# Two key-weight transfers of two rows, the first tile and the constants on another queue, and one low part ahead of another

## The chip, the core and the metric

The kernel runs on one core of a Trainium2 chip. The metric is the device time of one execution in microseconds, the median over the runs. A profiled execution is a run of its own, with its own time.

## What is computed

The input x has 2048 rows of 512. It is normalised row by row, and two branches work on the result xn:

```python
xn = layernorm(x)
# branch A: linear attention, 32 heads of 16
q, k, v = split(xn @ wqkv)
phi_q = [softmax(q @ w_phi), softmax(-q @ w_phi)]      # per head
phi_k = [softmax(k @ w_phi), softmax(-k @ w_phi)]
s = (phi_q @ (phi_k.T @ v)) / (phi_q @ sum(phi_k)) @ wo
# branch B: a gated feed-forward part, 1376 wide
g = silu((relu(xn @ W_gate) * (xn @ W_up)) @ W_down)
out = x + s * g
```

All of it is float32. Matrix products are made from high and low parts: a float32 operand is split into a part rounded to the fast matmul type and the rest, and three products (low times high, high times low, high times high) are added up. The function mm3 writes these three for each slice k of the contraction.

## The kernel before

The rows are taken in 16 tiles of 128. For each tile the kernel normalises, transposes (tile pxT, then XT in high and low part), and multiplies by the key, value and query weights (pk, pv, pq). All weights of the feed-forward branch and the second half of attention follow later; the change touches nothing of them.

Since w_phi acts per head, it is folded into the key and query weights at the start: fold(w, raw, k) multiplies row slice k of the transposed weight (wkT or wqT, tile wk_raw or wq_raw) by the block-diagonal constants bd_sb (named cb in the profile) on TensorE, four matmuls in the program, eight in the trace, into PSUM tile pfold. It returns a function that splits the outcome: ScalarE copies the high part (wkh), VectorE subtracts it for the low part (wkl). The four slices of the key weight are the four "rows" that this text speaks of; each row is 128 partitions of 512 numbers. In DRAM wkT is 128 x 4 x 512, so that a partition's rows lie behind each other, 8 KB in all.

The order of instructions on each engine is the order of the program; a helper (class InOrder, line 52) issues every one of them, which is why nearly all rows of the profile name L52. Transfers are issued by SyncE's queue (SPq) in program order, and each takes the semaphore of the eighth transfer before it, whose landing it waits for. GpSimd issues accumulating transfers on a queue of its own.

The start, lines 829 to 880, is written out by hand: first the loads, then norm_vector(0) with the statistics of the first tile (bs, bm, br on VectorE and GpSimd), the folds of key rows 0 and 1, norm_vector_apply(0) (xn), the split of row 0, the transposes of the first tile with its high part by ScalarE (turn(0, False)), the split of row 1, the folds of rows 2 and 3, then lo_xt, which subtracts on VectorE for the low part of XT, the remaining splits, the second tile's statistics between them, and the product pk of the first tile. In pk's order the first matmul of each slice reads the low part of XT with the high part of the weight; the second reads the high part of XT with wkl; the third both high parts.

Of the kernel before, what the change touches and what calls it, by code (L numbers as in the profile page):

```python
# [13 lines left out]
P = 128  # L14
# [5 lines left out]
KD = D // P  # L20
# [128 lines left out]
def layer_kernel(ctx: ExitStack, tc: tile.TileContext, x, wkT, wqT, wv, wo, wf, cst, out):  # L149
    pace = Clock()  # L150
    nc = InOrder(tc, pace)
# [7 lines left out]
    def u8(shape, name, dt=F32):  # L159
        return sb.tile(list(shape), dt, tag="u8", bufs=B8, name=name)  # L160
# [4 lines left out]
    def u2(shape, name, dt=F32):  # L165
        return sb.tile(list(shape), dt, tag="u2", bufs=B2, name=name)
# [7 lines left out]
    def f32(t):  # L174
        return t.bitcast(F32)

    def add(engine, o, a, b, op=ALU.add):
        engine.tensor_tensor(o, a, b, op=op)
# [31 lines left out]
    N = len(order)  # L210
    X = {}

    def load_x(n):
        b, i = order[n]
        t = b * TPB + i
        X[n] = u2((P, D), "xt")
        nc.sync.dma_start(X[n], x[t * P:(t + 1) * P, :])


    def w_tile(name):  # L220
# [5 lines left out]
    def fold(w, raw, k):  # L226

        p = ps(name="pfold")
        for j in range(KD):
            nc.tensor.matmul(p[:, j * P:(j + 1) * P], raw[:, j * P:(j + 1) * P], bd_sb[:, j, :],  # L230
                             start=True, stop=True)
        return lambda: split(*w[k], p)
# [44 lines left out]
    def transpose_x(n):  # L277
        p = ps((P, 2, 2, P), name="pxT")
        xn = XN.pop(n)
        for k in range(KD):  # L280
            transpose(p[:, k // 2, k % 2, :], xn[:, k * P:(k + 1) * P])
        return p

    def xt_parts(n, s):

        if n % 2 == 0:
            return [(XT[:, A11:A12 + 1, s, :, cols(n)], slice(0, 2))]
        if n not in A21:
            A21[n] = u2((P, 2, 2, P), "a21", F32R)
        return [(A21[n][:, s], 0), (XT[:, A22, s, :, cols(n)], 1)]  # L290

    def hi_xt(n, p):
        for to, c in xt_parts(n, 0):
            nc.scalar.activation(to, p[:, c], AF.Copy)

    def full_xt(n, p):
        XF[n] = u2((P, 2, 2, P), "xf")
        nc.scalar.activation(XF[n], p, AF.Copy)

    def lo_xt(n, p):  # L300
        for (to, c), (hi, _) in zip(xt_parts(n, 1), xt_parts(n, 0)):
            add(nc.vector, to, p[:, c], f32(hi), ALU.subtract)

    def turn(m, full=True):
        p = transpose_x(m)
        hi_xt(m, p)
        if full:
            full_xt(m, p)
        return m, p
# [519 lines left out]
    wk_raw, wv_raw, wq_raw = u8((P, KD, D), "wkT"), u8((P, KD, D), "wvr"), u8((P, KD, D), "wqT")  # L829
    bd_sb = u2((P, KD, P), "cb")  # L830
    ident = sb.tile([P, P], F32, name="ident")
    load_x(0)
    nc.sync.dma_start(bd_sb, cst[:, :KD, :])
    for k in range(KD):
        nc.sync.dma_start(wk_raw[:, k, :], wkT[:, k, :])
        if k == 0:
            nc.sync.dma_start(ident, cst[:, KD, :])
    load_x(1)
    nc.sync.dma_start(wq_raw[:, 0:2, :], wqT[:, 0:2, :])
    nc.sync.dma_start(wv_raw[:, 0:2, :], wv[:, 0:2, :])  # L840
    nc.sync.dma_start(wq_raw[:, 2:4, :], wqT[:, 2:4, :])
    load_x(2)
    nc.sync.dma_start(wv_raw[:, 2:4, :], wv[:, 2:4, :])
    for n in range(3, 7):
# [11 lines left out]
    norm_vector_apply(0)  # L856
    folds[0]()
    px = turn(0, False)
    folds[1]()
    folds = [fold(WK, wk_raw[:, k, :], k) for k in range(2, KD)]  # L860
    lo_xt(*px)
    folds[0]()
    norm_vector(1)
    folds[1]()
# [9 lines left out]
    px = turn(1)  # L874
# [288 lines left out]
```

## Time and profile before

| what | value |
|---|---|
| median of 3 runs | 585.73 us (585.71 to 586.2) |
| the profiled execution, own time | 586.47 us |
| its span, first to last instruction | 584.7 us |
| TensorE busy in the span | 572.5 us (98%) |
| VectorE, ScalarE, GpSimd busy | 395.4, 288.6, 390.2 us |
| SyncE's queue, moved | 125.66 MB |

In the profile PE is TensorE, PEld its weight loads, DVE VectorE, ACT ScalarE, POOL GpSimd, SP SyncE; a q behind an engine is its instruction queue, which issues transfers. Rows of a timeline give the start and the length in microseconds, then the operation as output<-inputs, and in brackets the idle time of that engine before it with what ended it. The chain of waits follows the work that ended last back from the last instruction.

### The profile page before, as it was taken

What the parts mean: (1) busy time and instruction counts of PE and PEld (TensorE: products, weight loads), DVE (VectorE), ACT (ScalarE), POOL (GpSimd) and SP (SyncE); (2) the same over time, 40 slices, a digit from 0 to 9 for tenths busy, and PEclk for the clock granted to TensorE, in tenths of its full rate; (3) what the DMA queues carried; (4) which work ended last, traced back from release to release, by engine and by line L of the source; (5) the groups of instructions that cost most, each with busy time, mean ns of one, the idle gap of its engine ahead of it and who ended that gap; (6) DMA issues with size and microseconds to landing.
All of it is one profiled execution on the core that took longest, in us unless ns stands there. A gap on an engine that the chain in (4) does not pass through costs nothing.

```text
span 584.7 us, 8483 instructions
## 1 busy us (share of the span) xinstructions
PE 572.5 (98%) x2764; PEld 478.0 (82%) x2764; DVE 395.4 (68%) x604; ACT 288.6 (49%) x529; POOL 390.2 (67%) x341
## 2 busy tenths in 40 slices
PE   4999999999999999999999999999999999999997
PEld 4788888888888888888888888888888888888886
DVE  2898765876647976787784532488788868673323
ACT  3798786864635356245434151153554545534510
POOL 0669987998866576997967342544457585775394
PEclk9999999999999999999999999999999999999999
DMA  8358897974698938978967999995576475669863
GB/s 289 112 150 223 221 307 233 265 222 126 164 279 272 347 95 261 301 263 293 283 215 226 319 389 398 315 390 193 130 266 170 137 227 169 183 206 275 254 176 113
DMA packets 82844, 138.26 MB, mean 236 GB/s; under 512 B 7664, under 2 KB 30576, under 8 KB 81904
## 3 DMA queue, kind: packets, MB, share of 16 engines
q1 hardware_dynamic: 79488, 125.66, 64.3%
q0 software_dynamic: 3312, 12.06, 10.8%
q8 instruction: 22, 0.36, 0.3%
q14 instruction: 22, 0.18, 0.1%
HBM read 77.14 MB, written 52.69 MB: 222 GB/s over the span
## 4 chain that ended last, share of the span: by engine, by line
PE 97%; DMA 1%; ACT 1%; DVE 1%; SPq 0%; issue 0%; POOL 0%; POOLq 0%
PE py L52 21%; PE pd L52 10%; PE pa L52 10%; PE pc L52 10%; PE pso L52 8%; PE pk L52 8%; PE pq L52 7%; PE pv L52 7%; PE pb L52 5%; PE pkv L52 3%; PE pnum L52 3%; PE ppT L52 2%; PE pxT L52 1%; PE pfold L52 1%; DMA wkT<-wkT 1%; PE pkb L52 0%
## 5 line engine op out<-in xcount | busy, mean ns | idle before, releaser
L52 PE MATMUL pa<-XT,wa 128*128 128x512 f32 x264 | 68.9, 393 | 0.0
L52 PE MATMUL py<-fdh,hl 128*128 128x512 f32 x176 | 68.8, 391 | 0.0
L52 PE MATMUL py<-fdh,hh 128*128 128x512 f32 x176 | 68.6, 390 | 0.0
L52 PE MATMUL py<-fdl,hh 128*128 128x512 f32 x176 | 68.5, 389 | 0.0
L52 POOL TENSOR_TENSOR hl<-e,hh 128x512 fp32r<-128x512 f32 x22 | 28.4, 1292 | 56.5 <-ACT hh L52 56.2
L52 PEld LDWEIGHTS pa<-XT,wa 128*128 128x128 f32 x264 | 48.5, 188 | 9.4
L52 ACT ACTIVATE hh<-e 128x512 fp32r<-128x512 f32 x22 | 13.9, 632 | 72.1 <-DVE e L52 67.4
L52 POOL TENSOR_TENSOR phl<-ek,phl 128x1024 fp32r<-128x1024 f32 x15 | 36.1, 2403 | 17.9 <-ACT phl L52 17.9
L52 POOL TENSOR_TENSOR hl<-u,hh 128x512 fp32r<-128x512 f32 x22 | 28.5, 1296 | 27.1 <-ACT hh L52 24.8
L52 DVE TENSOR_TENSOR y<-py,y 128x512 f32<-128x512 f32 x40 | 27.5, 689 | 27.2 <-PE py L52 27.1
L52 POOL TENSOR_TENSOR y<-y,ys 128x512 f32<-128x512 f32 x24 | 31.1, 1297 | 17.0 <-ACT ys L52 17.0
L52 PEld LDWEIGHTS py<-fdh,hh 128*128 128x128 f32 x176 | 33.0, 188 | 7.0
L52 PEld LDWEIGHTS py<-fdl,hh 128*128 128x128 f32 x176 | 33.0, 188 | 6.7
L52 PEld LDWEIGHTS py<-fdh,hl 128*128 128x128 f32 x176 | 33.1, 188 | 6.7
L52 POOL TENSOR_TENSOR ez<-eq,zB 128x1024 f32<-128x1024 f32 x16 | 38.4, 2405 | 0.0
L52 DVE TENSOR_TENSOR pTl<-ppT,pTh 128x512 fp32r<-128x512 f32 x32 | 22.1, 690 | 23.1 <-ACT pTh L52 22.7
L52 PE MATMUL pd<-XT,wd 128*128 128x512 f32 x132 | 34.9, 395 | 0.0
L52 PE MATMUL pd<-XT,wc 128*128 128x512 f32 x132 | 34.5, 392 | 0.0
L52 PE MATMUL pb<-XT,wb 128*128 128x512 f32 x132 | 34.5, 393 | 0.0
L52 PE MATMUL pc<-XT,wb 128*128 128x512 f32 x132 | 34.3, 391 | 0.0
L52 POOL TENSOR_TENSOR ol<-of,oh 128x1024 fp32r<-128x1024 f32 x8 | 19.4, 2431 | 22.2 <-ACT oh L52 15.3
L52 PE MATMUL pc<-XT,wc 128*128 128x512 f32 x132 | 34.1, 391 | 0.0
(163 smaller groups left out, 1632.8 us busy)
## 6 DMA issues: line engine op xcount, KB each, us to landing
zacc<-ek POOLq DMA_DIRECT2D x15, 512.0 KB, 5.2
xts<-XT SPq DMA_DIRECT2D x4, 1792.0 KB, 11.3
XT<-xts SPq DMA_DIRECT2D x7, 1024.0 KB, 15.8
wa<-ws SPq DMA_DIRECT2D x26, 256.0 KB, 5.3
wb<-ws SPq DMA_DIRECT2D x26, 256.0 KB, 5.3
wc<-ws SPq DMA_DIRECT2D x26, 256.0 KB, 4.9
rawg<-wf SPq DMA_DIRECT2D x22, 256.0 KB, 3.9
ws<-wa SPq DMA_DIRECT2D x22, 256.0 KB, 3.9
```

Of the source, the lines that this page charges most:

```text
L52: return self.tc.keep_in_program_order(op(*a, **k))
```

## The change

The key weights come in two transfers of two rows each (4 KB a partition) in place of four of one row (2 KB); they are now first on SyncE's queue. The first tile, the constants bd_sb and the identity are issued by ScalarE, in this order, ahead of its first own instruction. On VectorE, the low part of the first tile is put ahead of the low part of key row 1.

```diff
-    def load_x(n):
+    def load_x(n, queue=nc.sync):
...
-        nc.sync.dma_start(X[n], x[t * P:(t + 1) * P, :])
+        queue.dma_start(X[n], x[t * P:(t + 1) * P, :])
...
-    load_x(0)
-    nc.sync.dma_start(bd_sb, cst[:, :KD, :])
-    for k in range(KD):
-        nc.sync.dma_start(wk_raw[:, k, :], wkT[:, k, :])
-        if k == 0:
-            nc.sync.dma_start(ident, cst[:, KD, :])
+    load_x(0, nc.scalar)
+    for k in (0, 2):
+        nc.sync.dma_start(wk_raw[:, k:k + 2, :], wkT[:, k:k + 2, :])
+    nc.scalar.dma_start(bd_sb, cst[:, :KD, :])
+    nc.scalar.dma_start(ident, cst[:, KD, :])
     load_x(1)
...
     folds[0]()
     px = turn(0, False)
+    lo_xt(*px)
     folds[1]()
     folds = [fold(WK, wk_raw[:, k, :], k) for k in range(2, KD)]
-    lo_xt(*px)
     folds[0]()
```

By the order of instructions, TensorE's first matmul now waits for the first two-row transfer and for cb; its fifth in the program, which waited for a row of its own, waits no more. The fold of row 2 waits for the second two-row transfer. On VectorE one subtraction changes place with another; on ScalarE three transfer issues stand ahead of its table load; TensorE's order is the same.

## The prediction

> **What bounds the kernel now.** I read four views in this order: the page for the whole, a table of TensorE's busy time by stretch, the chain of waits through the start, and the timeline of the start with its transfers.
>
> ```profile
> span 584.7 us, 8483 instructions
> PE 97%; DMA 1%; ACT 1%; DVE 1%; SPq 0%; issue 0%; POOL 0%; POOLq 0%
> core 0: us, PE busy (x), PEclk, DMA share, GB/s
> 0.00:7.06 7.06, 0.00 (x1) 1.00 0.67 178
> 7.06:11.46 4.40, 4.40 (x21) 1.00 1.00 375
> 11.46:13.44 1.98, 1.98 (x17) 1.00 1.02 410
> 13.44:14.25 0.81, 0.00 (x2) 1.00 1.05 422
> 14.25:26.20 11.95, 11.20 (x68) 1.00 0.34 128
> 26.20:584.70 558.50, 554.94 (x2663) 1.00 0.76 238
> ```
>
> TensorE carries 97% of the chain that ended last. After 26.20 us it is idle for 558.50 - 554.94 = 3.56 us in all. So behind 26.20 the change, which edits only what comes before, can give nothing of its own; a shift of TensorE's work at 26 us is carried to the end, since what follows waits for events and not for the clock on the wall. TensorE's idle time ahead of that is 7.06 us before its first matmul, 0.81 us from 13.44 to 14.25, and 0.75 us later. The change works on the first two. The chain of waits says what ended them:
>
> ```profile
> 1.65 5.27 DMA wkT<-wkT
> 6.92 0.14 issue
> 7.06 3.75 PE pfold L52 x16
> ...
> 12.81 0.69 DVE wkl L52
> 13.51 0.61 DVE XT L52
> 14.11 0.14 issue
> 14.25 3.01 PE pk L52 x12
> ```
>
> The first gap ends with the landing of the first key-weight row, 5.27 us after its issue; TensorE starts 0.14 us later. The second ends with VectorE: it takes the weight row's low part (wkl) and only then the low part of the first tile (XT), and the product pk, whose first matmul reads that low part, starts 0.14 us after it.
>
> **The low part moved ahead (call it A).** The timeline, VectorE's and ScalarE's rows (start, length, what, idle time before and what ended it):
>
> ```profile
> 11.70 0.60 ACT L52 ACTIVATE XT<-pxT 128x512 fp32r<-128x512 f32 x1 [1.96 <-PE pxT L52]
> 12.19 1.08 ACT L52 ACTIVATE wkh<-pfold 128x512 fp32r<-128x512 f32 x2
> 12.81 0.69 DVE L52 TENSOR_TENSOR wkl<-pfold,wkh 128x512 fp32r<-128x512 f32 x1 [2.35 <-ACT wkh L52]
> 13.42 0.68 DVE L52 TENSOR_TENSOR XT<-pxT,XT 128x512 fp32r<-128x512 f32 x1
> 14.02 0.68 DVE L52 TENSOR_TENSOR wkl<-pfold,wkh 128x512 fp32r<-128x512 f32 x1
> 15.62 0.68 DVE L52 TENSOR_TENSOR wkl<-pfold,wkh 128x512 fp32r<-128x512 f32 x1
> 16.64 0.39 PE L52 MATMUL pk<-wkl,XT 128*128 128x512 f32 x1
> ```
>
> VectorE stood idle 2.35 us until 12.81, waiting for wkh of row 1. What XT's low part reads, its high part by ScalarE, was there at 11.70 + 0.60 = 12.30. Swapped, XT's low part runs from 12.32 to 13.00, and wkl of row 1 follows at 12.93 (operations there start 0.61 apart), where it was to start at 12.81 before: nothing is lost to that wait, and from 12.93 on VectorE's list (wkl of row 2, the second tile's statistics, wkl of row 3) runs 0.47 us earlier than now: 13.42 + 0.61 = 14.03 was the start of wkl of row 2, and becomes 13.54. With 13.00 + 0.14 = 13.14, pk no longer waits for VectorE; TensorE is done with the last fold at 13.44 and goes on at once. That takes the 0.81 us gap away. What is late next: the eleventh of pk's twelve matmuls reads wkl of row 3. It started at 16.64, 2.39 after pk's start, so is now due at 13.44 + 2.39 = 15.83. That wkl starts 0.47 earlier, at 15.15, ends at 15.83, and reaches TensorE 0.14 later, 15.97. So about 0.1 us is given back: A = 0.7 us. Between pk and 26 us ScalarE's copies hang on TensorE's folds and VectorE's operations on those, so they move along. Bounds for A: 0.47, if all that follows goes by VectorE's list, and 0.81.
>
> **The loads (B): when TensorE starts.** The issues, landings and rates of before; the column behind the size is the time from issue to landing, each transfer asked for alone in order of issue:
>
> ```profile
> xt<-x SPq DMA_DIRECT2D x1, 256.0 KB, 2.7
> cb<-cst SPq DMA_DIRECT2D x1, 256.0 KB, 2.9
> 1.18 0.42 SPq L52 DMA_DIRECT2D cb<-cst  x1
> DMA packets 259, 0.47 MB, mean 364 GB/s; under 512 B 28, under 2 KB 28, under 8 KB 259
> DMA packets 714, 1.12 MB, mean 233 GB/s; under 512 B 74, under 2 KB 202, under 8 KB 714
> DMA packets 229, 0.85 MB, mean 423 GB/s; under 512 B 19, under 2 KB 19, under 8 KB 229
> wqT<-wqT SPq DMA_DIRECT2D x2, 512.0 KB, 7.3
> DMA packets 253, 0.46 MB, mean 228 GB/s; under 512 B 30, under 2 KB 30, under 8 KB 253
> wor<-wo SPq DMA_DIRECT2D x1, 256.0 KB, 5.2
> ```
>
> The four rates are of the stretches 2.3 to 3.6 us (the tile and the constants), 3.6 to 8.4 (mostly the four key-weight rows), 9.5 to 11.5 (two-row loads of the query weights, issued between 3.6 and 8.4, and of the value weights with them) and 224.4 to 226.4 (a row of wo, cut like a key row, issued near 223 and landed 5.2 us later). One-row loads, 2 KB pieces 8 KB apart, move at 228 to 233 GB/s both times; two-row loads, 4 KB pieces with the same 8 KB between their starts, at 423. The layouts of wkT and wqT are the same, so I take 423 for the new key loads.
>
> Against that stands what must have landed before the first matmul: now the tile, the constants cb and one row; then cb and two rows, on two queues. How two queues share the engines is seen where GpSimd's accumulating transfer runs beside a spill on SyncE's queue, 104 to 106 us:
>
> ```profile
> q0 software_dynamic: 87, 0.36, 91.5%
> q1 hardware_dynamic: 85, 0.04, 10.7%
> ```
>
> 87 packets against 85, though those of q0 carry nine times the bytes: turns go by packet. So eight 4 KB packets of the first two rows alternate on each engine with eight 2 KB packets of the tile, and the next eight, of rows 2 and 3, with those of cb. The constants, second on ScalarE's queue, land only with the fourth row: after 4 x 0.262 MB of weights beside the 0.524 MB of tile and constants. Now cb lands at 1.18 + 2.9 = 4.08 with tile and constants alone ahead of it; then it lands at 4.08 + 1.049 MB / 423 GB/s = 6.56, and TensorE starts 0.14 later, at 6.70 instead of 7.06. B = 0.36 us. The constants, not the key rows, are then what it waits for.
>
> In the Trainium skill, "DMA: Bandwidth & Descriptors", section "Issuing engines are not separate DMA queues", says that transfers from several engines run on the same 16 DMA engines and interleave, and that a second issuer saves only issue time. The rows agree that they interleave; by that rule the second queue itself is worth nothing, and what gain there is comes from the longer pieces.
>
> B's bounds: if the two-row loads go at the 233 GB/s of one-row loads, cb lands at 4.08 + 4.50 = 8.58, the start is 8.72 and B = -1.66. If turns went by bytes instead, cb would wait for two rows only, 4.08 + 0.524 / 423 GB/s = 5.32, the start is 5.46 and B = +1.60. I stay near 0.36, as the 423 comes from the same layout on the same queue 5 us later.
>
> What else moves and costs nothing: the tile shares its turn with two rows and lands about 0.524 MB / 423 GB/s = 1.24 us later than its 0.75 + 2.7.
>
> ```profile
> 3.49 0.69 DVE L52 BATCH_NORM_STATS2 bs<-xt 128x6 f32<-128x512 f32 x1 [2.61 <-DMA xt<-x]
> 5.26 0.55 DVE L52 TENSOR_SCALAR xn<-xt,bm,br 128x512 f32<-128x512 f32 x1 [0.68 <-POOL br L52]
> 0.75 1.28 ACT L52 ACT_TABLE_LOAD   x1 [0.75 <-PEq L1155]
> 9.14 0.60 ACT L52 ACTIVATE wkh<-pfold 128x512 fp32r<-128x512 f32 x1 [7.11 <-PE pfold L52]
> ident<-cst SPq DMA_DIRECT2D x1, 64.0 KB, 5.0
> ```
>
> Its normalisation took from 3.49 to 5.81, so would end near 7.1, and the transposes that read it come 3.6 us after TensorE's start, at 10.3: 3 us of cover. The identity, third on ScalarE's queue, follows cb by eight short packets in turns with SyncE's, under 2 us, and is wanted at the same 10.3. Rows 2 and 3 are wanted 4.4 us after the start. ScalarE issues three transfers (about 0.45 us each, as SyncE's cb shows) before its table load, which then ends near 3.4; its first work is 2 us after TensorE's start. On SyncE's queue the later loads move up by five issues, and each transfer still waits for the eighth before it; those now land earlier, so the second tile and the query and value weights are not later than now.
>
> **The sum.** 0.7 + 0.36 = 1.06 us. The profiled execution took 586.47 us (its span 584.7 and 1.8 around it), so it would take 585.4; that execution lies 0.74 above the median of the plain runs, 585.73. Against the median: 584.7 us.
>
> **The rivals.**
> *The start gains nothing, A alone.* The first sixteen fold matmuls took 3.75 us and the next sixteen, from 11.46 to 13.44, 1.98, though the granted clock is printed as 1.00 for both. If that change of pace stays at its place in time, work pulled ahead by 0.36 us is done at half the pace, so B is worth 0.18 and the time is 584.85; if cb is late by 0.36 it is A alone, 585.0. In the Trainium skill, "TensorE: Matmul & The Clock Gate", section "Part 1: The HAM clock gate (the "warmup" mystery)", has a half clock at the start and a free-running window of about 3.4 us that ends it; by that rule the change of pace need not follow the start. The trace shows the two paces, not which of both holds. Chance 0.20.
> *The constants come late, slower.* Packets in turns put four rows ahead of cb, where one row was ahead of the start. Should the 233 GB/s of the key weights belong to this place and not to the 2 KB pieces, TensorE starts at 8.72 and the time is 585.73 + 1.66 - 0.7 = 586.7. It decides once TensorE starts later than 7.06 + 0.7 = 7.76. For it: 3.6 to 8.4 is the only stretch of key rows. Against it: the wo row, in another place, at 228, and the two-row loads at 423. Chance 0.17.
> *Turns by bytes, or cb early.* TensorE starts at 5.46: 585.73 - 0.7 - 1.60 = 583.4. The 87 to 85 packets speak against it. Chance 0.08.
> *It does nothing at the end*, because VectorE or GpSimd hold the stretch up to 26 us: 585.7. For it: GpSimd and VectorE take turns there; against it: ScalarE's and VectorE's rows there wait for TensorE's folds. Chance 0.05.
>
> **How the numbers follow.** The forecast has 0.50, with its own range 584.2 to 585.2 (B from 0.1 to 0.8, A from 0.5 to 0.8). About what a measurement of this kernel can tell from no change is 0.2%, 1.17 us: faster means under 584.56. The forecast lies just short of it; I give faster three fifths of its half, 0.30, as packets of two queues may overlap a little, and add the 0.08 of the early constants: 0.38. Slower, over 586.90, is most of the late constants, since 586.7 is close to it, and little else: 0.12. The rest, 0.50, is within. The range leaves out the far ends of the early and the late case: 583.5 to 586.6.
>
> **What would show it.** In the changed profile, TensorE's first fold starts at 6.7, right behind a landing of cb, not of wkT; the issues' table has wkT from issue to landing at under 5.5 us for 512 KB; VectorE's order is XT, wkl, wkl with no wait of pk on VectorE's XT, and the gap of 0.81 us ahead of pk is under 0.15; pk of the second tile starts near 25.1 instead of 26.2, and the rest of TensorE's rows keep their lengths. The forecast is wrong if the first fold starts past 7.8, if pk's gap stays, or if the idle time after 26 us differs from 3.6 us by more than half a microsecond.

## The result and the profile after

The changed kernel took 587.02 us (median of 13 runs, 586.37 to 587.97). The kernel before, run beside it, took 586.2 us (13 runs, 584.78 to 586.67); the 585.73 us told above is the median of the first three of these. The ratio is 1.002, with a 95% interval of 1.0012 to 1.0028: slower, and above the predicted range of 583.5 to 586.6. The profiled execution took 587.09 us with a span of 585.3, against 586.47 and 584.7.

The chain of waits of the changed kernel through the start (start, length, what):

```profile
1.18 6.78 DMA cb<-cst
7.96 0.14 issue
8.09 3.76 PE pfold L52 x16
11.85 0.85 PE pxT L52 x4
12.70 1.87 PE pfold L52 x16
14.57 2.30 PE pk L52 x10
16.87 0.04 issue
16.91 0.73 PE pk L52 x2
17.64 1.80 PE pfold L52 x16
```

TensorE starts at 8.09 us where it started at 7.06, and now the constants cb release it, not a weight row. From there on everything is quicker: pk of the first tile follows the folds with no wait, and ends at 17.64, 9.55 us after the first fold; before it ended at 17.26, 10.20 us after. So the start lost 1.03 us and the low part won 0.65.

The timeline of the changed kernel shows the new order on VectorE and what pk waits for now:

```profile
5.95 0.69 DVE L52 BATCH_NORM_STATS2 bs<-xt 128x6 f32<-128x512 f32 x1 [5.08 <-DMA xt<-x]
13.37 0.69 DVE L52 TENSOR_TENSOR XT<-pxT,XT 128x512 fp32r<-128x512 f32 x1 [1.87 <-ACT XT L52]
13.97 1.28 DVE L52 TENSOR_TENSOR wkl<-pfold,wkh 128x512 fp32r<-128x512 f32 x2
16.18 0.68 DVE L52 TENSOR_TENSOR wkl<-pfold,wkh 128x512 fp32r<-128x512 f32 x1
16.91 0.19 PEld L52 LDWEIGHTS pk<-wkl,XT 128*128 128x128 f32 x1 [0.46 <-DVE wkl L52]
26.59 0.48 PE L52 MATMUL pk<-wkh,a 128*128 128x512 f32 x1
```

XT's low part comes first. The wait that is left is the one of the eleventh matmul, on wkl of row 3, at 16.91. The second tile's pk starts at 26.59 instead of 26.20. Behind it nothing changed, as the row of TensorE's stretches shows (busy time in the second number; idle 558.71 - 555.04 = 3.67 us, before 3.56):

```profile
core 0: us, PE busy (x), PEclk, DMA share, GB/s
26.59:585.30 558.71, 555.04 (x2663) 1.00 0.75 237
```

The transfers of the changed kernel: the rate from 2.3 to 3.6 us, with the two queues' packets (q1 is SyncE's, q10 ScalarE's), then the rates from 3.6 to 5.0 and from 5.0 to 6.5; then the issues in order, with the time from issue to landing behind the size.

```profile
DMA packets 114, 0.36 MB, mean 280 GB/s; under 512 B 0, under 2 KB 0, under 8 KB 114
q1 hardware_dynamic: 64, 0.26, 68.3%
q10 hardware_dynamic: 50, 0.10, 26.5%
DMA packets 152, 0.40 MB, mean 287 GB/s; under 512 B 21, under 2 KB 21, under 8 KB 152
DMA packets 217, 0.62 MB, mean 416 GB/s; under 512 B 16, under 2 KB 16, under 8 KB 217
wkT<-wkT SPq DMA_DIRECT2D x1, 512.0 KB, 5.0
wkT<-wkT SPq DMA_DIRECT2D x1, 512.0 KB, 6.4
xt<-x ACTq DMA_DIRECT2D x1, 256.0 KB, 5.2
cb<-cst ACTq DMA_DIRECT2D x1, 256.0 KB, 6.8
```

64 packets of one queue beside 50 of the other carry 0.26 and 0.10 MB: turns go by packet, and the queue with the longer pieces gets the bytes. cb, with the tile ahead of it on its queue, lands 6.8 us after its issue, where it took 2.9 before. In the stretch in which the first two rows and the tile should have moved at 423 GB/s, the rate was 280, and 287 up to 5.0 us. From there it was 416, while the second pair of rows, which lies in DRAM like the first, was still moving.

### The profile page after: what moved, and what is told of

It is laid out like the page before. It is cut to its first block, busy times and chain, and to the rows that moved or that the text cites. A ratio compares the mean times of both kernels' runs of the same rounds, so it can differ in the third digit from the quotient of the medians.

```text
span 585.3 us, 8477 instructions
## 1 busy us (share of the span) xinstructions
PE 572.7 (98%) x2764; PEld 478.4 (82%) x2764; DVE 395.4 (68%) x604; ACT 288.5 (49%) x529; POOL 390.2 (67%) x341
## 4 chain that ended last, share of the span: by engine, by line
PE 97%; DMA 1%; ACT 1%; DVE 1%; POOL 0%; issue 0%; ACTq 0%; POOLq 0%
PE py L52 21%; PE pa L52 10%; PE pd L52 10%; PE pc L52 10%; PE pso L52 8%; PE pk L52 8%; PE pq L52 7%; PE pv L52 7%; PE pb L52 5%; PE pkv L52 3%; PE pnum L52 3%; PE ppT L52 2%; PE pfold L52 1%; DMA cb<-cst 1%; PE pxT L52 1%; PE pkb L52 0%
```

## The experiments

Fourteen kernels were run. For each: the median and that of the kernel before beside it, the ratio, and from its profile the start of TensorE's first fold and of the second tile's pk. From that pk to the end of the span every profile has 558.45 to 558.78 us, so the last column stands for the whole of the profiled execution. That is one execution and need not be a middle one: e4's took 587.96 us, the longest of its eleven. The experiments ran on four chips, so a difference between two of them is best read through the kernel before beside each.

| kernel | us | before | ratio (95%) | first fold | second pk |
|---|---|---|---|---|---|
| changed | 587.02 | 586.2 | 1.002 (1.0012 to 1.0028) | 8.09 | 26.59 |
| e1 low part alone | 585.39 | 586.07 | 0.9989 (0.998 to 0.9998) | 5.95 | 24.44 |
| e2 loads alone | 587.68 | 586.07 | 1.0027 (1.0016 to 1.0038) | 8.68 | 27.56 |
| e3 constants first | 585.73 | 586.07 | 1.0005 (0.9996 to 1.0015) | 6.04 | 25.14 |
| e4 one queue | 586.82 | 586.07 | 1.0017 (1.0009 to 1.0026) | 9.00 | 27.50 |
| e5 rows contiguous | 584.34 | 586.02 | 0.997 (0.9958 to 0.9981) | 6.12 | 24.72 |
| e6 rows padded | 584.17 | 586.02 | 0.9967 (0.9954 to 0.9979) | 5.94 | 23.86 |
| e7 pairs contiguous | 585.79 | 586.02 | 0.9995 (0.9986 to 1.0004) | 7.34 | 25.74 |
| e8 rows, two queues | 586.23 | 586.02 | 1.0 (0.9991 to 1.0008) | 7.46 | 25.95 |
| e9 tile after row | 583.72 | 585.79 | 0.9962 (0.9949 to 0.9975) | 4.28 | 23.08 |
| e10 pairs, one queue | 586.16 | 585.79 | 1.0003 (0.9995 to 1.0012) | 7.79 | 26.27 |
| e11 tiles ahead | 588.36 | 585.79 | 1.0041 (1.0029 to 1.0053) | 9.73 | 28.21 |
| e12 constants on SyncE | 584.41 | 585.79 | 0.997 (0.9959 to 0.9981) | 5.66 | 24.16 |
| e13 pairs padded | 586.56 | 585.77 | 1.0013 (1.0004 to 1.0022) | 7.63 | 26.43 |
| e14 changed again | 587.24 | 585.77 | 1.0023 (1.0014 to 1.0032) | 8.09 | 26.54 |

### The two parts, each alone

e1 is the kernel before with the low part moved:

```diff
     px = turn(0, False)
+    lo_xt(*px)
     folds[1]()
     folds = [fold(WK, wk_raw[:, k, :], k) for k in range(2, KD)]
-    lo_xt(*px)
```

> The loads as before, only the first tile's low part ahead of the low part of key row 1. Theory (the reordering gains, the loads lose more): TensorE starts at 7.0 to 7.1 as before, the gap of 0.81 us ahead of pk is under 0.15, and from the first fold to the end of pk it takes 9.55 us as in the changed kernel, where before took 10.20; the second tile's pk starts near 25.6; the time is 0.65 us under before. Rival (the reordering is lost or hurts, because the last matmuls of pk now wait for row 3's low part): the second tile's pk starts at 26.2 or later and the time is that of before or above.

e2 is the changed kernel with that undone:

```diff
     px = turn(0, False)
-    lo_xt(*px)
     folds[1]()
     folds = [fold(WK, wk_raw[:, k, :], k) for k in range(2, KD)]
+    lo_xt(*px)
```

> The loads as in the changed kernel, the low parts in the order of before. Theory (the loads cost): TensorE starts near 8.1, behind the landing of the constants, 1.0 us later than before; the gap of 0.8 us ahead of pk is there again; the second tile's pk starts near 27.2 and the time is 1.0 to 1.5 us over before. Rival (the loss came from elsewhere, from the reordering or from the second queue by itself): start near 8.1 but a time within 0.4 us of before, or a start near 7.1.

The chain of waits of e1, and its rate from 3.6 to 8.4 us:

```profile
5.95 3.75 PE pfold L52 x16
9.70 0.85 PE pxT L52 x4
10.56 2.09 PE pfold L52 x16
12.64 2.85 PE pk L52 x12
15.50 1.80 PE pfold L52 x16
DMA packets 798, 1.25 MB, mean 261 GB/s; under 512 B 95, under 2 KB 223, under 8 KB 798
```

pk ends 15.50 - 5.95 = 9.55 us after the first fold, as in the changed kernel. The low part alone is worth 0.65 us by the profiles and 586.07 - 585.39 = 0.68 by the medians. The loads alone cost 587.68 - 586.07 = 1.61, somewhat over the 1.0 to 1.5 that was expected, and in e2's chain the wait ahead of pk is back:

```profile
1.18 7.37 DMA cb<-cst
14.18 0.69 DVE wkl L52
14.87 0.61 DVE XT L52
```

The two parts are two effects with opposite signs. e1 also shows how far one profile can be trusted: its loads are those of the kernel before, and its first fold is at 5.95, not 7.06.

### The order on ScalarE's queue

e3 is the changed kernel with the constants ahead of the tile.

```diff
-    load_x(0, nc.scalar)
+    nc.scalar.dma_start(bd_sb, cst[:, :KD, :])
+    load_x(0, nc.scalar)
...
-    nc.scalar.dma_start(bd_sb, cst[:, :KD, :])
```

> The changed kernel, but on ScalarE's queue the constants go ahead of the first tile. Theory (turns by packet: the constants were late because all four key rows were ahead of them): the constants land with the first two rows, at 5.0 to 5.8, TensorE starts at 5.2 to 6.0; the first tile now lands where the constants did, near 8.0, its normalisation ends near 10.3, and the transposes, wanted 3.6 us after the start, wait for it by 0.5 to 1.5 us; the time is 0.5 to 1.5 us under before. Rival (the start of the transfers is slow whatever comes first): the constants land past 7, and the time is that of the changed kernel or above.

The tile in its chain of waits, and two rows of its timeline:

```profile
1.18 6.78 DMA xt<-x
6.04 3.78 PE L52 MATMUL pfold<-cb,wkT 128*128 128x128 f32 x16 [6.04 <-DMA cb<-cst]
10.37 0.89 PE L52 MATMUL pxT<-ident,xn 128*128 128x128 f32 x4 [0.54 <-DVE xn L52]
```

With one transfer less ahead of cb, TensorE starts 2.05 us earlier; the tile, now second, lands at 1.18 + 6.78 = 7.96 by its chain, exactly where cb landed in the changed kernel, and the transposes wait 0.54 us for it. The median is 1.29 under the changed kernel's, and 0.34 under the kernel before beside it, where 0.5 to 1.5 was expected. Its twelve runs lie in two groups, eight at 585.39 to 585.9 and four at 587.12 to 587.56; the profile is of the first, and what parts them is not known. In the profile the lateness belongs to the second place on ScalarE's queue, whatever stands there.

### One queue or two, one row or two

e4 puts all on SyncE's queue in the order of before, with two-row transfers and the low part moved. e8 is the changed kernel with four one-row transfers.

```diff
 e4, against e1
-    for k in range(KD):
-        nc.sync.dma_start(wk_raw[:, k, :], wkT[:, k, :])
+    for k in (0, 2):
+        nc.sync.dma_start(wk_raw[:, k:k + 2, :], wkT[:, k:k + 2, :])
 e8, against the changed kernel
-    for k in (0, 2):
-        nc.sync.dma_start(wk_raw[:, k:k + 2, :], wkT[:, k:k + 2, :])
+    for k in range(KD):
+        nc.sync.dma_start(wk_raw[:, k, :], wkT[:, k, :])
```

> All loads on SyncE's queue again in the order of before, the key rows in two transfers of two rows, the low parts in the changed order. Theory (order on two queues is to blame, two-row pieces are as fast as those of the query weights, 423 GB/s): the constants land at 4.1 as before, the first two rows at 5.3, TensorE starts at 5.5, the time is 1.6 + 0.65 = 2.2 us under before. Rival (key rows that lie 8 KB apart are slow when they come first, in pieces of 2 or of 4 KB: 233 to 257 GB/s as in both kernels until 4.6 to 8 us): the first two rows land at 6.1 to 6.5, TensorE starts at 6.3 to 6.7 and the time is 1.0 to 1.4 us under before. Should two rows in one transfer make the first fold wait for more than they save, it starts at 7.06 or later and the time is 0.6 under before at the most.

> The changed kernel with its two queues, but the key rows come in four transfers of one row, 2 KB pieces 8 KB apart. Theory (turns go by packet): eight packets of the tile and eight of the constants alternate with eight of row 0 and eight of row 1, so the constants land with the second row, at half the weight bytes of the changed kernel: 5.6 if nothing is slow, 6.2 to 7.2 with the slow start seen so far; TensorE starts 0.14 later and the time is 0.2 to 1.2 us under before, and in any case under that of the changed kernel. Rival (turns by bytes, or the second queue itself delays the constants): the constants land past 7.4 and the time is that of the changed kernel.

The chain of waits of e4, its rate from 4 to 6 us, and the chain of e8:

```profile
1.66 7.20 DMA wkT<-wkT
DMA packets 99, 0.30 MB, mean 149 GB/s; under 512 B 6, under 2 KB 29, under 8 KB 99
```

```profile
1.18 6.15 DMA cb<-cst
```

With e1 and the changed kernel that makes a square, all four with the low part moved: 585.39 (one queue, one row), 586.82 (one queue, two rows), 586.23 (two queues, one row), 587.02 (both). Two rows in one transfer cost 1.43 us on one queue and 0.79 on two; the second queue costs 0.84 with single rows and 0.20 with pairs. Against the kernel before beside each, the four are -0.68, 0.75, 0.21 and 0.82 us, so the costs become 1.43, 0.61, 0.89 and 0.07. The pairs are a loss by themselves, as the intervals show on one queue and on two. The second queue with single rows probably is one too (the intervals of e1 and e8 overlap by a hair); with pairs it costs nothing that can be seen. e4 came out as the last of its three cases, a start past 7.06 and no more than 0.6 us gained. In e8 the constants landed at 1.18 + 6.15 = 7.33, between what theory and rival had; it beats the changed kernel, but the gain over the kernel before did not come. e4 has no second queue, so TensorE waits for the weights: twice the bytes must land before the first fold, and they moved at 149 GB/s.

### The layout of the key weights in DRAM

Is it the place in time or the layout that makes them slow? In e5 each row (of e1's loads) lies contiguous in DRAM; in e6 the 2 KB pieces lie 8704 bytes apart instead of 8192; e7 is the changed kernel with each pair of rows contiguous; e10 is e4 with contiguous pairs; e13 is the changed kernel with its 4 KB pieces 8704 bytes apart, and e14 the changed kernel again beside it. The host only stores the same numbers elsewhere.

```diff
 e5
-        nc.sync.dma_start(wk_raw[:, k, :], wkT[:, k, :])
+        nc.sync.dma_start(wk_raw[:, k, :], wkT[k])
 e6
+        nc.sync.dma_start(wk_raw[:, k, :], wkT[:, k, :D])
 e7, e10
+        nc.sync.dma_start(wk_raw[:, k:k + 2, :], wkT[k // 2])
 e13
+        nc.sync.dma_start(wk_raw[:, k:k + 2, :].rearrange("p k d -> p (k d)"), wkT[:, k // 2, :2 * D])
```

> The loads and queue of before, the low parts in the changed order, but wkT lies in DRAM row after row: each of the four transfers reads 256 KB in one piece instead of 128 pieces of 2 KB that start 8 KB apart. Theory (the 8 KB between the pieces makes the start slow: in before, the changed kernel and the one-queue kernel alike the key rows move at 170 to 260 GB/s until some 5 to 8 us): the first row lands at 4.7 to 5.0, 3.2 us after its issue instead of 4.2 to 5.3, TensorE starts at 4.9 to 5.2, from 3.6 to 8.4 us the rate is 380 to 420 GB/s, and the time is 2.4 to 2.8 us under before (1.9 to 2.1 from the start, 0.65 from the low part). Rival (the place is slow, first transfers after the constants, whatever they read): the first row lands at 5.8 to 6.9 as in the two kernels with one-row loads, the rate stays at 230 to 260 GB/s, and the time is 0.7 under before.

> As the kernel with contiguous rows, but wkT keeps its layout with every row padded by 128 bytes: the pieces are 2 KB as in before and start 8704 bytes apart instead of 8192. Theory in its narrow form (it is the round distance of 8192, under which all pieces of a row fall in the same place of some pattern of the memory): as contiguous, first row landed at 4.7 to 5.0, TensorE started at 4.9 to 5.2, time 2.4 to 2.8 us under before. Theory in its wide form (any scattered pieces are slow): first row landed at 5.8 to 6.9, time 0.7 under before. The constants, whose 2 KB pieces start 4608 bytes apart, landed without delay, which speaks for the narrow form.

> The changed kernel with its two queues, but wkT lies in DRAM as two pairs of rows, each pair 512 KB in one piece. Theory (two faults of the forecast are apart: the order of turns put the constants behind all four rows, and that was foreseen at 1.57 MB and full rate; the slow start of rows 8 KB apart was not): the constants land with the last rows at 6.2 to 6.7 and TensorE starts at 6.3 to 6.8, as forecast for the changed kernel; the time is 0.9 to 1.4 us under before. Rival (two queues at the start are slow by themselves): the constants land past 7.4 and the time is that of before or above.

> All loads on SyncE's queue in the order of before, key rows in two transfers of two rows, low parts in the changed order, and wkT in DRAM as two contiguous pairs. Theory (two rows in one transfer cost for two reasons that can be told apart: the first fold waits for twice the bytes, some 0.65 us at full rate, and the scattered rows were slow in that kernel, 170 GB/s at 4 to 6 us): the first pair lands at 5.4 to 6.2, TensorE starts at 5.5 to 6.4, the time is 1.0 to 2.0 us under the one-queue kernel with scattered pairs (586.8), so 584.8 to 585.8. Rival (the slow start is not of the layout): TensorE starts past 7, time 586.3 or more.

> The changed kernel with its two queues, the pairs of rows still in 4 KB pieces, but these start 8704 bytes apart instead of 8192. Theory (the round distance of 8192 is what made the changed kernel's start slow): constants landed near 7.2 and TensorE started near 7.3, as with contiguous pairs on two queues; over 300 GB/s from 2.3 to 3.6 us; time 1.0 to 1.4 us under the changed kernel run beside it. Rival (pieces that are scattered at all are slow): constants landed near 8, TensorE started near 8.1, under 290 GB/s from 2.3 to 3.6 us, time within 0.4 us of the changed kernel.

> The changed kernel as it is, beside the padded one on the same chip. All theories: constants landed at 7.6 to 8.3, TensorE started at 7.8 to 8.4, time 0.7 to 1.2 us over before.

The medians fall in every pair: e1 to e5 by 1.05 us, e1 to e6 by 1.22, changed to e7 by 1.23, e4 to e10 by 0.66, e14 to e13 by 0.68. Against the kernel before beside each, that is 1.00, 1.17, 1.05, 0.38 and 0.68. The 0.38 of e10 is not shown, as its interval overlaps that of e4; e13 and e14 ran side by side on one chip, and e14's median lies above the highest run of e13. The rates, in the order e5 and e6 (3.6 to 8.4 us), e7 (2.3 to 3.6), e13 (2.3 to 3.6, then 3.6 to 5.0), e10 (4 to 6):

```profile
DMA packets 855, 1.40 MB, mean 291 GB/s; under 512 B 94, under 2 KB 222, under 8 KB 855
```

```profile
DMA packets 843, 1.36 MB, mean 284 GB/s; under 512 B 92, under 2 KB 220, under 8 KB 843
```

```profile
DMA packets 153, 0.48 MB, mean 365 GB/s; under 512 B 0, under 2 KB 0, under 8 KB 153
```

```profile
DMA packets 111, 0.35 MB, mean 269 GB/s; under 512 B 0, under 2 KB 0, under 8 KB 111
DMA packets 217, 0.58 MB, mean 414 GB/s; under 512 B 31, under 2 KB 31, under 8 KB 217
```

```profile
DMA packets 238, 0.57 MB, mean 285 GB/s; under 512 B 22, under 2 KB 110, under 8 KB 238
```

Contiguous pairs went at 365 where scattered ones went at 280, and on one queue at 285 where e4 had 149. The padded pairs of e13 were still slow up to 3.6 us (269) and then went at 414, where the changed kernel had 287; the start came 0.46 us sooner (7.63 against 8.09), and the 0.68 us lie between what the two theories expected. e14 itself came to 1.47 over the kernel before, above the 0.7 to 1.2 that was expected.

The rows of e5 and e6, in pieces of 2 KB, gained only 261 to 291 and 284, far from the full rate that was expected of them; two profiles of the old layout, before and e1, are themselves 28 apart (233 and 261). Their times fell by 1.7 to 1.9 us against the kernel before, not by 2.4 to 2.8. e7 started at 7.34 instead of 6.3 to 6.8 and gained 0.23 us on the kernel before instead of 0.9 to 1.4. e10 fell outside what was expected too: its first fold came at 7.79 and it was no faster than before. So a layout without 8 KB between the pieces is worth 0.7 to 1.2 us in four of the five pairs, but it explains only a part of the slow start.

In the Trainium skill, "DMA: Bandwidth & Descriptors", section "Latency and other measured facts", tells of copies slowed by row pitches that are large powers of two, from 512 KiB on, and restored by 4 KiB of padding, though not by 192 B. The gains of e6 and e13 at a pitch of 8 KiB, with 512 B of padding, agree in sign; the rate came back to 414 GB/s in e13 and not in e6.

### The place in time

e11 is e1 with four tiles of x loaded between the constants and the first row, so that the rows come later.

```diff
     nc.sync.dma_start(bd_sb, cst[:, :KD, :])
+    for n in range(1, 5):
+        load_x(n)
...
-    load_x(1)
...
-    load_x(2)
...
-    for n in range(3, 7):
+    for n in range(5, 7):
```

> As the kernel with the low part alone, but four more tiles of x (contiguous, 1.05 MB) are loaded between the constants and the first key row. Theory (the slowness belongs to the key rows): from 3.6 to 6 us the tiles move at 380 GB/s or more, and the key rows that follow are slow in their turn, 230 to 290 GB/s, wherever they stand; TensorE starts at 8.5 to 9.5. Rival (it belongs to the time, the first 3 to 8 us of an execution): the tiles are slow, under 300 GB/s from 3.6 to 6, and the key rows after 7 us go at 380 or more. The time itself, 2 to 3 us over the low part alone, tells little.

Its rates from 3.6 to 6 us (tiles), from 6 to 9 (the last tile, then key rows) and from 7 to 8.5 (key rows and the identity):

```profile
DMA packets 415, 0.76 MB, mean 317 GB/s; under 512 B 44, under 2 KB 44, under 8 KB 415
DMA packets 489, 0.74 MB, mean 248 GB/s; under 512 B 54, under 2 KB 150, under 8 KB 489
DMA packets 192, 0.26 MB, mean 172 GB/s; under 512 B 18, under 2 KB 82, under 8 KB 192
```

The key rows, in the later stretch, are no faster: 172 once the tiles are through. In their old place the tiles, cut into pieces of 2 KB as well, move at 317, above the key rows and yet under the 380 that a pure effect of layout should have shown. The start at 9.73 us is past the 8.5 to 9.5 that was expected. Neither explanation is enough: rows of the old layout are slow here at 7 to 8.5 us, so the place alone does not make them slow, and the second pair of the changed kernel, in the old layout, was in a stretch of 416 from 5.0 us on, so the layout alone does not either.

### Two better starts

Both use e6's padded rows. e9 keeps one queue, puts the constants first and the tile behind the first row; e12 puts only the tile and the identity on ScalarE's queue and leaves the constants first on SyncE's.

```diff
 e9
-    load_x(0)
     nc.sync.dma_start(bd_sb, cst[:, :KD, :])
     for k in range(KD):
         nc.sync.dma_start(wk_raw[:, k, :], wkT[:, k, :D])
         if k == 0:
+            load_x(0)
+        if k == 1:
             nc.sync.dma_start(ident, cst[:, KD, :])
```

```diff
 e12
-    load_x(0)
+    load_x(0, nc.scalar)
...
-        if k == 0:
-            nc.sync.dma_start(ident, cst[:, KD, :])
+    nc.scalar.dma_start(ident, cst[:, KD, :])
```

> One queue, four rows padded to 8704 bytes apart, the changed order of the low parts; the constants and the first row are issued first, then the first tile, then row 1 and the identity. Theory (TensorE's start is set by the bytes ahead of the last of constants and first row): 0.524 MB instead of 0.786, so the first row lands 0.5 to 0.7 us earlier than in the padded kernel (5.8 there in the profile, about 5.2 by its median), TensorE starts at 4.3 to 5.2, the normalisation of the tile ends near 7.5, under the 3.6 us that the folds take; time 0.4 to 0.7 under the padded kernel, 583.5 to 583.8, or 2.2 to 2.6 under before. Rival (the scattered row is slow wherever it stands, and as second transfer it is as slow as the key rows of the changed kernel at their start): first row at 5.2 to 6, time as the padded kernel or above.

> Two queues, but the constants go first on SyncE's queue, ahead of the four rows (padded, one row a transfer); ScalarE's queue has only the first tile and the identity; low parts in the changed order. Theory (in turns by packet the constants now alternate with the tile only, and row 0 follows with the queue to itself): TensorE starts as in the padded kernel on one queue, 5.2 to 6.0, time 584.0 to 584.6; the second queue by itself neither gains nor costs. Rival (two queues at the start are slow by themselves): start past 6.5, time 585.2 or more.

Of e9, the chain of waits and, from the timeline, the row of xn:

```profile
1.19 2.96 DMA wkT<-wkT
4.28 4.07 PE pfold L52 x16
8.35 0.85 PE pxT L52 x4
7.24 0.55 DVE L52 TENSOR_SCALAR xn<-xt,bm,br 128x512 f32<-128x512 f32 x1 [0.68 <-POOL br L52]
```

TensorE starts at 4.28, with constants and one row ahead of it and nothing else; xn is done at 7.79, still ahead of the transposes at 8.35. 583.72 us is the best of all the versions and beats both kernels; that it beats e6 is not shown, as their intervals overlap. e12 starts at 5.66. With nothing on the second queue that the first matmul wants, its harm is gone within what the intervals tell (e12 against e6), but nothing here shows a gain in time from it. Its rate from 3.6 to 6.5 us was 386 GB/s, where e6 had 284 for pieces of the same cut; why is open, as the two ran on different chips and the order of their loads differs.

## Why the prediction was wrong

*What bounds the kernel*: right. TensorE's idle time after the second tile's pk moved by 0.1 us, and from there on all kernels take the same time within 0.33 us.

*A, the low part*: right. The forecast was 0.7 us, measured were 0.65 and 0.68. The 0.81 us wait is gone, and the give-back came where it was said: the eleventh matmul of pk waits for wkl of row 3, 16.91 - 8.09 = 8.82 us after the first fold; the forecast had 15.97 - 7.06 = 8.91.

*B, who ends the wait*: right. Turns by packet put the four rows ahead of cb, and cb releases TensorE; e3 shows it by changing the order.

*B, how long it lasts*: this is the step that failed. The prediction took "423 for the new key loads", from two-row loads at 9.5 to 11.5 us, and so had cb at 4.08 + 1.049 MB / 423 GB/s = 6.56. It landed at 7.96: B is -1.03 us in this pair of profiles instead of +0.36. Two terms of that sum were off.

The first is the rate. The transfers moved at 280 and 287 GB/s up to 5.0 us and at 416 only from there. The 0.77 MB from 2.3 to 5.0 took 2.70 us, where 423 would have taken 1.82: by this estimate, 0.88 us. It is the same in the other profile of the changed kernel, e14 (284, 290, then 412). Padded pairs (e13) reach 414 from 3.6 us, and contiguous pairs (e7) take the start from 8.09 to 7.34, so 0.75 of the 1.39 us of lateness goes with the layout, which the argument had declared harmless for 4 KB pieces. Why the scattered pieces are slow only until 5.0 us stays open.

The second is the bytes. The sum let SyncE's queue move four rows beside cb and no more. But SyncE's transfer of the second tile stands behind the rows and takes turns with cb too. That queue's packets begin at 1.78 us, ScalarE's at 2.18, and when the last packet of cb started, at 7.37, 94 of SyncE's had been pieces of the second tile. This is what its queue had moved by then (packets, MB):

```profile
q1 hardware_dynamic: 388, 1.25, 50.2%
```

The 0.20 MB over 1.049 take 0.48 us at 416 GB/s, again an estimate; with the 0.88 it makes 1.36 of the 1.40 us by which cb was late. In e7 the queue had moved 1.22 MB when cb's last packet started, at 6.66, which is some 0.4 of the 0.64 us that remain there.

*The size against the medians.* e2 says that the loads cost 1.61 us, more than the 1.03 of that pair of profiles. The kernel before was measured with its first fold at 7.06, but the same loads in e1 gave 5.95; the changed loads gave 8.09, 8.09 and 8.68. So the trace of before probably held a late landing of the first row; the prediction took its 7.06 as the kernel's start, and one profile cannot say so. With 1.6 lost and 0.7 won the sum is +0.9, and +0.82 was measured; the second comparison (e14) has +1.47.

*The rivals.* "The constants come late, slower" came true: its condition, a start past 7.76, holds at 8.09, and its price of -1.66 for the start is near the loads' 1.61, in part by luck: it takes a start at 8.72 and a start before at 7.06, where the starts seen are 8.09 to 8.68 and, for the old loads, 5.95 to 7.06. Nor were 233 GB/s a fact of the place, as the rate rose to 416 there. It had a chance of 0.17, because the slow rows of wo, in another place, were read as "short pieces are slow" and not as "this layout is slow". "Turns by bytes" is refuted by the packets. "The start gains nothing" as worded is refuted too, since the start lost; but its reason, the change of pace, is partly seen. The chains of e1 and of e6 begin within 0.01 us of each other, and their second pk is 0.58 apart. e6's chain:

```profile
5.94 3.61 PE pfold L52 x16
9.55 0.45 PE pxT L52 x4
23.86 0.47 PE L52 MATMUL pk<-wkh,a 128*128 128x512 f32 x1
```

The transposes take 0.45 us here and 0.85 in e1: the faster pace begins earlier. By the single matmuls of folds and transposes, which go from 421 to 275 ns, the first shorter one starts 3.1 us after the first fold in e6, 4.6 in the changed kernel, 5.0 in e1 and 5.4 in e9. The sixteen folds of e9 take 4.07 us instead of 3.75 for another reason, a wait for row 1 at the ninth of them, which starts 0.36 us after the eighth where 0.21 is usual and holds up the tenth in turn; its second pk came 18.80 us after the first fold, in e1 18.49. The printed clock is 1.00 in all of them. The Trainium skill, "TensorE: Matmul & The Clock Gate", section "Part 1: The HAM clock gate (the "warmup" mystery)", has a window of some 3.4 us that does not begin with the kernel; that the pace changes at unequal distances agrees with it.

*What else moved*: the tile came later than forecast (statistics at 5.95 instead of about 4.7) and its cover held, as the transposes came only at 11.85. The key transfers took 5.0 and 6.4 us where "under 5.5" was asked for.

## What to carry to other kernels

Count, in the order in which the queues take turns, the bytes that stand ahead of the operand that lands last for the first matmul; a queue with longer pieces takes more of the rate, it goes on with its next transfer, and a small tensor behind other loads on a second queue pays. Put that operand first and ask for no more bytes in its transfer than the first instruction needs. A rate is a fact of one layout at one place, so one from 5 us later is a bound, not a value; and a start read from one profile should be read from a second one before it goes into a sum.

## What the runs showed of the hardware

While pieces of 4 KB that lie 8 KB apart were loaded, the rate was 149 GB/s (e4, 4 to 6 us), 280 (changed, 2.3 to 3.6, beside the tile) and, for the rest of the same weights, 416 (changed, 5.0 to 6.5); the same cut of other weights was at 423 at 9.5 us. With the pieces 8704 bytes apart it was 414 from 3.6 us (e13). The landing of the first key row, with the same loads and issued within 0.02 us of the same time, came 5.27 us after its issue in one profile and 4.15 in another. And TensorE's change of pace is not tied to its first matmul: it came 3.1 to 5.4 us after it in four profiles, and with starts at 5.94 and 5.95 the second pk was 0.58 us apart some 18 us later.
